# Mamba-2 scan and ELU feed-forward on one core: weight pieces spread over three steps, ELU first in each step, wide decays for two blocks, an earlier turn

## The chip, the cores and the metric

The kernel runs on one core of one Trainium2 chip. The metric is the device time of one execution in microseconds (us). Below, PE is the matrix engine (PEld its weight loads), DVE, ACT and POOL are the vector, scalar and GpSimd engines, and SP issues most DMAs.

## The reference

Two operations one after the other, in float32. The first is a chunked state-space scan over 4 batches, 8 heads, 768 tokens, head size 32 and state size 16; the second is a feed-forward layer with ELU over 3072 tokens (256 to 2048 to 256):

```python
cum = np.cumsum(la, axis=-1)                      # la = log(a) in one chunk
L = np.exp(cum[:, :, :, None] - cum[:, :, None, :]) * causal
M = np.einsum('bhin,bhjn->bhij', Cc, Bc) * L
y[:, :, sl] = einsum(M, xc) + einsum(Cc, state) * np.exp(cum)[..., None]
state = decay_full * state + sum over j of Bc_j xc_j * decay_from_j
...
x = y.transpose(0, 2, 1, 3).reshape(3072, 256)
h = x @ w_in
g = np.where(h > 0.0, h, np.exp(np.minimum(h, 0.0)) - 1.0)
out = g @ w_out
```

The two weights reach the kernel as 64-bit floats, and it makes 32-bit ones of them itself.

## The kernel before

**Blocks.** The 3072 tokens are 12 blocks of 256 (`n` = 0 to 11), each with all 8 heads of a batch. Inside a block the scan goes by chunks of 64 tokens. All four engines' orders are written out by hand: an instruction stands in its engine's queue where the Python text emits it, and nothing reorders it.

**The scan of a block** has these parts: `spread_cum` (a DMA puts the running sums of `log a` into the tile `L`, two buffers), `decay_of` (L516: per head two ACT exponentials of 128x64 with a bias from `ncum`, the negative running sum by token; after four heads two POOL selects cut the half above the diagonal away), `scaled` (POOL: B times its decay), `turn` (L421: four transposes on PE, one copy on ACT, then on DVE the masked C, `ctm`) and `turn_exp` (DVE), `scores` (PE, four PSUM tiles), `sums` (PE, two PSUM tiles), `weigh` (DVE: M = scores times `L`), `states` (DVE steps `S_new`, each followed by a POOL product `Sx`), `across` (PE, from `Sx`) and `inside` (PE, from M and x; then six copies into `yT`, the layer's input).

**The layer.** Blocks 0 to 3 go through `l1(n, i)` (L655): four passes that make two hidden tiles of 128 features times 256 tokens in one PSUM tile. `elu()` (L682) takes the oldest of these: `Relu` and `Exp` on ACT (L680, L687), then one DVE operation that writes `g` (L689). The PSUM tile is free when that has run. `l2(n, j)` (L817) multiplies `g` with `w_out`. From hidden tile 8 of blocks 2 and 3 on, pairs of blocks go through `l1_words(n, m)` (L778), in which inputs and weights are split in words (`words_of_y`, `both_of_y`, `words_of_w`, `low_of_w`): six passes into two PSUM tiles, `high` (from y1 and y0) and `both` (from `y_both`), and the second layer is done by `second`, a generator that `l2s(count)` advances.

**PSUM.** Seven of eight banks belong to one pool, whose tiles are handed out in the order of the text; which released tile a new one takes, and so what PE waits for, follows from that order.

**Weight pieces.** There are 16 (0 to 7 are `w_in`, 8 to 15 are `w_out`). Each goes through `w_abs` (ACT), `w_low` (ACT or DVE), `w_sign` (DVE), `w_high` (two DVE operations, L231 and L238) and `w_sum` (POOL, L248). `w_take` is the first three, `w_give` the last two.

**The two loops that the change rewrites.** The twelve-step loop (L1092 to L1134, `s` = 0 to 11) runs `l1(1, 0..7)` and `l1(0, 4..7)`, makes pieces 5 to 10 (each whole at one odd step, its `w_low` on DVE), exponentiates block 2's decays one head per step, turns block 2 at step 5, takes its scores and sums at step 7 and its `across` and `inside` at step 10, and calls `elu()` at the end of each step for the tile of the step before. The eight-step loop (L1173 to L1221, `j` = 0 to 7) runs `l2(0, j)` and `l1(2, 0..3)`, then `l1(3, 0..3)`, makes pieces 11 to 15 (one a step at j = 0, 2, 3, 4, 5: `w_take` before `l1`, `w_give` after it, then `elu()`), finishes block 3 (states at j = 2, `across` at j = 3) and begins blocks 4 and 5 (`scan_ahead`). It ends with `words_of_y(2)` at j = 4 and `both_of_y(2)` at j = 5. A loop of `l1_words(2, 8..15)` follows, and then one of 16 steps for each pair from block 4 on.

Of the kernel before, what the change touches and what calls it, by code (L numbers as in the profile page):

```python
# [17 lines left out]
P = 128  # L18
Q = 64
# [13 lines left out]
def kernel(  # L33
# [406 lines left out]
    def turn_exp(n, eng=nc.vector):  # L440

        s = st[n]
        s["cts"] = s["squares"][:, 1]
        eng.tensor_tensor(out=s["cts"], in0=s.pop("ct"), in1=s["ec"], op=ALU.mult)
# [68 lines left out]
    def decay(n, q):  # L513

        decay_of(n, 2 * q)
        decay_of(n, 2 * q + 1)  # L516

    def decay_of(n, h):
        L, row = st[n]["L"], rows_of(n).start + NG * h
        for u in range(2):  # L520
            nc.scalar.activation(  # L521
                L[:, h, u], L[:, h, u], ACT.Exp, bias=ncum[:, u, row:row + 1])
        if h % 4 == 3:
            for v in range(2):
                part = L[Q * v:Q * v + Q, h - 3:h + 1]
                nc.gpsimd.affine_select(  # L526
                    out=part, in_=part, pattern=[[0, 4], [0, 2], [1, Q]],
                    compare_op=ALU.is_ge, fill=0.0, base=0, channel_multiplier=-1)

# [218 lines left out]
    def words_of_y(n):  # L750

        y = yT[n // 2].rearrange("p k b u i -> p k (b u i)")
        y1 = conv.tile([P, KC, 2 * BLK], F32R, tag="y1", name="y1", bufs=1)
        y0 = conv.tile([P, KC, 2 * BLK], F32R, tag="y0", name="y0", bufs=1)
        nc.scalar.activation(y1[:, 1], y[:, 1], ACT.Copy, scale=NEAR / WORD)
        if n == 4:
            nc.scalar.activation(y1[:, 0], y[:, 0], ACT.Copy, scale=NEAR / WORD)
        else:
            nc.vector.tensor_scalar(
                out=y1[:, 0], in0=y[:, 0], scalar1=NEAR / WORD, scalar2=None, op0=ALU.mult)  # L760
        for k in range(KC):
            nc.vector.scalar_tensor_tensor(
                out=y0[:, k], in0=y1[:, k].bitcast(F32), scalar=WORD, in1=y[:, k],
                op0=ALU.mult, op1=ALU.subtract)
        y_words[n] = y1, y0
# [11 lines left out]
    def l1_words(n, m, between=None):  # L777

        cols = slice(m % 2 * P, (m % 2 + 1) * P)
        w, w0 = k_words[m // 2]  # L780
        w1, both_w, w0 = w[:, 0, :, cols], w[:, 1, :, cols], w0[:, :, cols]
        y1, y0, both_y = y_words[n]
        high, both = psum([P, 2 * BLK], "ps_h"), psum([P, 2 * BLK], "ps_w")
        passes = [(high, w1, y1), (high, w0, y0), (both, both_w, both_y)]
        for ps, lhs, rhs in passes if n > 2 and m == 0 else passes[2:] + passes[:2]:
            for k in range(KC):
                nc.tensor.matmul(  # L787
                    out=ps, lhsT=lhs[:, k], rhs=rhs[:, k], start=k == 0 and lhs is not w0,
                    stop=k == KC - 1 and lhs is not w1)
        if between:  # L790
            words_of_y(between)
        e = ffn.tile([P, 2 * BLK], F32, tag="e", name="e", bufs=2)
        nc.scalar.activation(e, both, ACT.Copy, scale=WORD)  # L793
        if late:
            end_words()
        nc.vector.scalar_tensor_tensor(  # L796
            out=high, in0=high, scalar=WORD - 1.0, in1=e, op0=ALU.mult, op1=ALU.add)
        late.append((n, m, high, e))
# [167 lines left out]
    def w_take(i, low):  # L966

        w_abs(i)
        w_low(i, low)
        w_sign(i)  # L970

    def w_give(i):

        w_high(i)
        w_sum(i)
# [112 lines left out]
    w_load(10)  # L1088
    write_flat(2)

    todo = 5
    for s, (n, i) in enumerate((  # L1092
            (1, 0), (1, 1), (1, 2), (0, 4), (1, 3), (0, 5), (1, 4), (0, 6), (1, 5), (0, 7),
            (1, 6), (1, 7))):
        l1(n, i, parts=2 if s < 2 else 1)
        if s < 8:
            decay_of(2, s)
        if s == 7:
            st[0] = kept
            scores(2)  # L1100
            sums(2, 0, pool=p_o, tag="o", parts=(None, last))
            weigh(2, 0)
            weigh(2, 1)
        if s % 2 == 1 and todo < 11:
            w_take(todo, nc.vector)
            w_give(todo)
            w_load(todo + 6)
            todo += 1
        if s in (1, 3):
            load_bc(3, us=(s // 2,))  # L1110
        if s == 9:
            write_flat(0)
        if s == 4:
            scaled(2, nc.gpsimd)
        if s == 5:
            turn(2)
            turn_exp(2)
        if s == 4:
            load_x(3)
            spread_exp(3)  # L1120
        if s == 8:
            weigh(2, 2)
            weigh(2, 3)
            states(0, last)
            st.pop(0)
            states(2)
        if s == 9:
            decay(3, 0)
            decay(3, 1)
        if s == 10:  # L1130
            spread_cum(4)
            inside(across(2), 2)
        if len(lag) > 1:
            elu()  # L1134


    def weigh_two(m, q):
# [35 lines left out]
    for j in range(2 * DIRECT):  # L1173
        n, i = 2 + j // DIRECT, j % DIRECT
        if j < 7:
            l2(0, j)
        piece = todo < len(pieces) and j != 1
        if j == 0:
            elu()
        if piece:  # L1180
            w_take(todo, nc.vector)
        l1(n, i)
        if j == 7:
            l2(0, j)
        if j == 0:
            scaled(3, nc.gpsimd)
            turn(3)
            elu()
            turn_exp(3)
        if piece:  # L1190
            w_give(todo)
            todo += 1
        while lag:
            elu()
        if j == 0:
            decay(3, 2)
            decay(3, 3)
        if j == 1:
            scores(3)
            sums(3)  # L1200
            for q in range(4):
                weigh(3, q)
        if j == 2:
            states(3)
        if j == 3:
            inside(across(3), 3)
        if j == 4:
            words_of_y(2)
        if j == 4:
            words_of_w(4)  # L1210
        if j == 5:
            low_of_w(4)
        if j == 5:
            both_of_y(2)
        scan_ahead(j)
        if j == 3:
            s_out[:] = weight_sums()
        if j == 6:
            differences(0, 4)
        if j == 7:  # L1220
            words_of_w(5)  # L1221
    for j in range(8, 16):
        i = j - 8
        l1_words(2, j)
        if i == 7:
            words_of_y(4)
        for p in ((), (6,), (), (7,), (0,), (1,), (2,), ())[i]:
            words_of_w(p)
        for p in ((5,), (), (6,), (7,), (0,), (), (), ())[i]:
            low_of_w(p)  # L1230
        if i == 7:
            l2(1, 6)
            l2(1, 7)
        begin_end()
        if i == 0:
            turn_part(5, 2)
            scaled(4, nc.gpsimd)
            scaled(5, nc.gpsimd)
        if i < 2:
            load_bc(i + 6)  # L1240
            l2(1, i)
        if i == 2:
            turn_part(4, 3)
            turn_part(5, 3)
            scores(4, 5)
            sums(4, 5)
            for q in range(4):
                weigh_two(4, q)
            l2(1, 2)
            states(4)  # L1250
            states(5)
            for to in (6, 7):
                load_b(to)
                spread_cum(to)
        if i == 3:
            l2(1, 3)
        if i == 4:
            y = across(4, 5)
            l2(1, 4, half=0)
            inside(y, 4, 5, ts=(0,))  # L1260
            l2(1, 4, half=1)
            inside(y, 4, 5, ts=(1,))
        if i == 5:
            l2(1, 5)
        if i in (0, 1, 3, 4):
            sum_t1(2, (0, 1, 3, 4).index(i), nc.vector)
        if i in (4, 6):
            turn_part(6, i // 2 - 2)
        if i in (2, 5):
            differences(4 if i == 2 else 6, 2)  # L1270
        if i < 6:
            sum_weights(nc.gpsimd, a_out, s_out, i)
# [30 lines left out]
    for n in range(4, NP, 2):  # L1303
# [3 lines left out]
        def l2s(count):  # L1307
            for _ in range(count):
                next(steps)

        for k in range(16):
# [13 lines left out]
            if not m:  # L1325
                l2s(4 if k % 2 else 3)
                continue
            l2s((3 + (n == 4), 3 - (n == 4), 3, 3, 3, 3, 3, 3, 4, 5, 2, 2, 3, 1, 2, 0)[k])
            if k == 9:
                scores(m, m + 1)  # L1330
                sums(m, m + 1)
# [5 lines left out]
                states(m + 1)  # L1337
            if k == 13:
                y = across(m, m + 1)
                l2s(1)  # L1340
                inside(y, m, m + 1, ts=(0,))
                l2s(2)
                inside(y, m, m + 1, ts=(1,))
        if m:
            l2s(4)
# [39 lines left out]
```

## Time and profile before

| what | us |
|---|---|
| median of 3 runs (349.99 to 350.6) | 350.07 |
| the profiled execution, its own time | 350.85 |
| its span | 349.1 |
| PE busy | 339.9 |
| DVE / ACT / POOL busy | 259.0 / 234.7 / 216.8 |
| twelve-step loop and the one product after it, 27.5 to 53.7: span, PE, ACT busy | 26.2, 26.19, 24.04 |
| from there to the end of step j = 7's `l1`, 53.7 to 81.5: span, PE, ACT busy | 27.8, 27.80, 23.87 |
| words of blocks 2 and 3, 81.5 to 117.7: span, PE, DVE busy | 36.2, 34.56, 32.35 |

Times in the profile count from the start of the span. A row of the timeline gives start and duration in us, then engine, line, operation, written tile <- read tiles, sizes and how many such instructions were merged; in square brackets, how long the engine sat idle before, and what ended that. Durations of neighbouring instructions of one engine overlap a little, so the distance from start to start (the pitch) is what one costs in a full queue.

### The profile page before, as it was taken

To read this page: it belongs to the slowest core of one execution; us is meant where nothing else is said; L and a number is where in the kernel's file an instruction comes from. 1 tells how busy PE (TensorE), PEld (TensorE's weight loads), DVE (VectorE), ACT (ScalarE), POOL (GpSimd) and SP (SyncE) were. 2 spreads that over 40 slices of the span, in tenths; PEclk is the share of its full clock that TensorE was granted. 3 is DMA by queue.
4 is the path that set the end of the run, shared out by engine and by line. 5 is a ranking of instruction groups with operands and counts; after the bars stand their busy time and mean duration, and the time that the engine had idled before them with its cause. 6 is when DMAs were issued, how large, how long until landed. Compare 5 with 4: busy or idle time off the path is not lost.

```text
span 349.1 us, 9873 instructions
## 1 busy us (share of the span) xinstructions
PE 339.9 (97%) x3878; PEld 297.5 (85%) x3878; DVE 259.0 (74%) x515; ACT 234.7 (67%) x537; POOL 216.8 (62%) x338
## 2 busy tenths in 40 slices
PE   7889999998999999999999999999999999999996
PEld 4669888887777889988999988989988999999996
DVE  4898988879997889875878775888675756665232
ACT  5689989597748889657699447699557466565000
POOL 5554554566999599984196764196854174455760
PEclk9999999999999999999999999999999999999999
DMA  8878988470261331070431070320000100001002
GB/s 145 220 220 180 303 175 252 95 132 31 66 126 23 91 62 32 8 151 15 106 62 32 8 160 4 99 40 2 2 0 5 62 0 3 0 0 56 9 0 62
DMA packets 72727, 26.49 MB, mean 76 GB/s; under 512 B 57768, under 2 KB 67560, under 8 KB 72680
## 3 DMA queue, kind: packets, MB, share of 16 engines
q1 hardware_dynamic: 70360, 25.60, 31.4%
q8 instruction: 30, 0.49, 0.6%
q10 hardware_dynamic: 2320, 0.26, 0.5%
q14 instruction: 17, 0.14, 0.1%
HBM read 22.51 MB, written 3.34 MB: 74 GB/s over the span
## 4 chain that ended last, share of the span: by engine, by line
PE 87%; DVE 3%; DMA 3%; SPq 3%; ACT 1%; issue 1%; POOL 1%; DVEq 0%; POOLq 0%; ACTq 0%
PE ps_o L904 36%; PE ps_h L787 18%; PE ps_h L667 11%; PE ps_w L787 9%; PE ps_o L829 6%; PE ps_y L634 3%; DMA w<-in_moe_w_in_dram 2%; PE ps_g L541 2%; PE ps_y L616 2%; PE ps_st L571 1%; DMA bc<-in_C_dram 1%; DVE y_both L772 1%; SPq L116 1%; SPq L178 1%; PE ps_o L890 1%
## 5 line engine op out<-in xcount | busy, mean ns | idle before, releaser
L904 PEld LDWEIGHTS ps_o<-w_out,g 128*128 128x128 f32 x640 | 78.5, 191 | 3.5
L904 PE MATMUL ps_o<-w_out,g 128*128 128x128 f32 x640 | 80.1, 275 | 0.0
L802 ACT ACTIVATE e<-ps_h 128x512 f32<-128x512 f32 x72 | 43.0, 598 | 50.5 <-DVE ps_h L796 50.5
L810 DVE SCALAR_TENSOR_TENSOR g<-e,ps_h 128x512 f32<-128x512 f32 x72 | 49.3, 685 | 31.1 <-ACT e L803 30.8
L845 POOL TENSOR_TENSOR g<-g 128x256 f32<-128x256 f32 x36 | 26.5, 737 | 57.3 <-DVE g L810 57.2
L796 DVE SCALAR_TENSOR_TENSOR ps_h<-ps_h,e 128x512 f32<-128x512 f32 x72 | 50.1, 695 | 13.1 <-ACT e L793 10.0
L793 ACT ACTIVATE e<-ps_w 128x512 f32<-128x512 f32 x72 | 42.3, 587 | 15.0 <-PE ps_w L787 14.9
L787 PE MATMUL ps_w<-y_both,w_words 128*128 128x512 f32 x144 | 51.5, 437 | 0.1
L667 PE MATMUL ps_h<-yT,w_in 128*128 128x256 f32 (+1 forms) x208 | 45.2, 368 | 2.5 <-POOL w_in L248 1.6
L803 ACT ACTIVATE e<-e 128x512 f32<-128x512 f32 x72 | 45.5, 632 | 2.3
L787 PE MATMUL ps_h<-y,w_words 128*128 128x512 f32 x144 | 45.6, 398 | 0.0
L787 PE MATMUL ps_h<-y,w 128*128 128x512 f32 x144 | 45.0, 392 | 0.2 <-POOL w L845 0.2
L667 PEld LDWEIGHTS ps_h<-yT,w_in 128*128 128x128 f32 x208 | 36.3, 190 | 8.4 <-POOL w_in L248 3.6
L521 ACT ACTIVATE L<-L,ncum 128x64 f32<-128x64 f32 x160 | 42.2, 336 | 0.2
L904 PE MATMUL ps_o<-w_sum,g 128*128 128x128 f32 x304 | 38.6, 276 | 0.0
L904 PEld LDWEIGHTS ps_o<-w_sum,g 128*128 128x128 f32 x304 | 37.0, 192 | 1.3
L526 POOL TENSOR_SCALAR_AFFINE_SELECT L<-L 64x512 f32<-64x512 f32 x40 | 29.2, 731 | 9.6 <-ACT L L521 7.5
L787 PEld LDWEIGHTS ps_h<-y,w 128*128 128x128 f32 x144 | 27.0, 188 | 7.1 <-POOL w L845 0.7
L787 PEld LDWEIGHTS ps_h<-y,w_words 128*128 128x128 f32 x144 | 26.7, 188 | 6.2 <-issue 0.5
L829 PE MATMUL ps_o<-w_out,g 128*128 128x256 f32 x128 | 30.9, 384 | 1.0 <-POOL w_out L248 1.0
L845 POOL TENSOR_TENSOR g<-t,g 128x256 f32<-128x256 f32 x40 | 28.1, 734 | 5.8 <-PE ps_o L904 5.7
L845 POOL TENSOR_TENSOR g<-g,t 128x256 f32<-128x256 f32 x40 | 28.7, 747 | 0.2
(133 smaller groups left out, 535.9 us busy)
## 6 DMA issues: line engine op xcount, KB each, us to landing
L<-flat SPq DMA_DIRECT2D x20, 256.0 KB
w<-in_moe_w_out_dram SPq DMA_DIRECT2D x8, 512.0 KB
w<-in_moe_w_in_dram SPq DMA_DIRECT2D x7, 512.0 KB
xr<-in_x_dram SPq DMA_DIRECT2D x24, 128.0 KB
out_dram<-c_sum SPq DMA_DIRECT2D x9, 256.0 KB
bc<-in_B_dram SPq DMA_DIRECT2D x24, 64.0 KB
bc<-in_C_dram SPq DMA_DIRECT2D x22, 64.0 KB
ec<-flat_exp SPq DMA_DIRECT2D x10, 128.0 KB
```

The source lines that it names most:

```text
L521: nc.scalar.activation(L[:, h, u], L[:, h, u], ACT.Exp, bias=ncum[:, u, row:row + 1])
L526: nc.gpsimd.affine_select(out=part, in_=part, pattern=[[0, 4], [0, 2], [1, Q]], compare_op=ALU.is_ge, fill=0.0, base=0, channel_multiplier=-1)
L667: nc.tensor.matmul(out=ps[:, j, toks], lhsT=w_in[i][:, k, j * P:(j + 1) * P], rhs=yT[n // 2][:, k, n % 2].rearrange("p u i -> p (u i)")[:, ...
L787: nc.tensor.matmul(out=ps, lhsT=lhs[:, k], rhs=rhs[:, k], start=k == 0 and lhs is not w0, stop=k == KC - 1 and lhs is not w1)
L793: nc.scalar.activation(e, both, ACT.Copy, scale=WORD)
L796: nc.vector.scalar_tensor_tensor(out=high, in0=high, scalar=WORD - 1.0, in1=e, op0=ALU.mult, op1=ALU.add)
L802: nc.scalar.activation(e, high, ACT.Relu, scale=-1.0)
L803: nc.scalar.activation(e, e, ACT.Exp, scale=-1.0)
L810: nc.vector.scalar_tensor_tensor(out=g_of[n, m].rearrange("p b i -> p (b i)"), in0=e, scalar=1.0, in1=h, op0=ALU.subtract, op1=ALU.max)
L829: nc.tensor.matmul(out=o_of[n][:, ts], lhsT=g_of[n, j][:, m % 2, ts * P:(ts + 1) * P], rhs=w_out[:, m], start=(m == 0 and ts == 0), stop=( ...
L845: nc.gpsimd.tensor_tensor(out=out, in0=in0, in1=in1, op=ALU.subtract)
L904: nc.tensor.matmul(out=ps[:, ts], lhsT=b[:, ts * P:(ts + 1) * P], rhs=a[:, i], start=(i == chunk[0] and ts == 0), stop=(i == chunk[-1]), s ...
```

## The change

It edits eight places:

- Pieces 5 to 10 are spread over three steps: `w_abs` and `w_sign` at an even step, `w_low` (on ACT instead of DVE) and `w_high` at the next, `w_sum` at the one after.
- In the twelve-step loop `elu()` comes right behind `l1`, ahead of everything else of the step.
- Blocks 2 and 3 get their decays in halves of four heads: a POOL addition of `ncum` over 128x512 (`from_token`), one ACT exponential of 128x512 (`wide_exp`), and the two POOL selects (`mask`), each a step apart. Block 2's run from before step 0 to step 3, block 3's from step 7 to 11.
- Block 2's `turn` and `turn_exp` move from step 5 to step 4, behind `scaled`.
- In the eight-step loop pieces 11 to 15 come whole behind `elu()`, with `w_low` on ACT; piece 15 moves from j = 5 to j = 4.
- `words_of_y` has both halves of y1 on ACT for n = 2 as well as n = 4.
- `l1_words` does `both` last at m = 15 and, for n = 2, at m = 8; `words_of_y(4)` moves into `l1_words(2, 15)`, ahead of its evacuation.
- Some `l2` and `l2s` calls around `inside` are regrouped; their number stays.

```diff
+    def from_token(n, half, eng=nc.gpsimd):
+        part = st[n]["L"][:, 4 * half:4 * half + 4]
+        first_row = rows_of(n).start + 4 * NG * half
+        eng.tensor_tensor(
+            out=part, in0=part,
+            in1=ncum[:, :, first_row:first_row + 4 * NG:NG].rearrange(
+                "p u h -> p h u").unsqueeze(3).to_broadcast([P, 4, 2, Q]), op=ALU.add)
+    def wide_exp(n, half):
+        part = st[n]["L"][:, 4 * half:4 * half + 4]
+        nc.scalar.activation(part, part, ACT.Exp)
...
-        nc.scalar.activation(y1[:, 1], y[:, 1], ACT.Copy, scale=NEAR / WORD)
-        if n == 4:
-            nc.scalar.activation(y1[:, 0], y[:, 0], ACT.Copy, scale=NEAR / WORD)
-        else:
+        for k in (0, 1) if n < 6 else (1,):
+            nc.scalar.activation(y1[:, k], y[:, k], ACT.Copy, scale=NEAR / WORD)
+        if n > 5:
...
-        for ps, lhs, rhs in passes if n > 2 and m == 0 else passes[2:] + passes[:2]:
+        for ps, lhs, rhs in passes if m == (8 if n == 2 else 0) or m == 15 else passes[2:] + passes[:2]:
...
+    def step(s):
+        for n, at in ((2, -1), (3, 7)):
+            for half in range(2):
+                if s == at + 2 * half + 2:
+                    mask(n, half)
+                if s == at + 2 * half:
+                    from_token(n, half)
+                if s == at + 2 * half + 1:
+                    wide_exp(n, half)
+    def convert(s):
+        p = 5 + s // 2
+        if s % 2 == 0 and s > 0:
+            w_sum(p - 1)
+        if s % 2 == 0 and p < 11:
+            w_abs(p)
+            w_sign(p)
+        if s % 2 == 1:
+            w_low(p, nc.scalar)
+            w_high(p)
+            w_load(p + 6)
+    step(-1)
...
         l1(n, i, parts=2 if s < 2 else 1)
-        if s < 8:
-            decay_of(2, s)
+        if len(lag) > 1:
+            elu()
+        step(s)
...
-        if s % 2 == 1 and todo < 11:
-            w_take(todo, nc.vector)
-            w_give(todo)
-            w_load(todo + 6)
-            todo += 1
+        if s == 4:
+            scaled(2, nc.gpsimd)
+            turn(2)
+            turn_exp(2)
+        convert(s)
...
-        if s == 9:
-            decay(3, 0)
-            decay(3, 1)
...
-        if len(lag) > 1:
-            elu()
...
         if j == 0:
+            w_sum(10)
             elu()
-        if piece:
-            w_take(todo, nc.vector)
         l1(n, i)
...
-        if piece:
-            w_give(todo)
-            todo += 1
         while lag:
             elu()
-        if j == 0:
-            decay(3, 2)
-            decay(3, 3)
+        for p in {0: (11,), 2: (12,), 3: (13,), 4: (14, 15)}.get(j, ()):
+            w_take(p, nc.scalar)
+            w_give(p)
...
-        l1_words(2, j)
-        if i == 7:
-            words_of_y(4)
+        l1_words(2, j, between=4 if i == 7 else None)
...
-            l2(1, 4, half=0)
             inside(y, 4, 5, ts=(0,))
-            l2(1, 4, half=1)
+            l2(1, 4)
...
-                l2s(1)
                 inside(y, m, m + 1, ts=(0,))
-                l2s(2)
+                l2s(4)
```

In the last loop the entry for k = 14 in the list of `l2s` counts goes from 2 to 1.

## The prediction

> **What bounds the kernel now.** I read the page first, then what PE waited for, then the timeline of each stretch that the change touches. The page gives PE 97% busy and 87% of the chain that ended last, and PEclk 9 in every slice. So the end moves only by what PE waits, and the wait list says how little that is.
>
> ```profile
> PE 87%; DVE 3%; DMA 3%; SPq 3%; ACT 1%; issue 1%; POOL 1%; DVEq 0%; POOLq 0%; ACTq 0%
> PE ps_h L667 <- POOL w_in L248: 1.6, 3, 0.8
> PE ps_o L829 <- POOL w_out L248: 1.0, 1, 1.0
> ```
>
> All three waits for `w_in` end by 23.3 us, ahead of the change. From 27.5 on the only long one is 1.0 us for piece 15 of `w_out`. The change can win that and a few tenths more; it loses whatever new wait it makes. So I put the new order of each queue against PE's pace: 1.73 us for an `l1` or an `l2` (53.72 to 55.45 in PE's timeline).
>
> The twelve-step loop, timeline of all engines (ACT's rows from 14 us for `w_low`):
>
> ```profile
> 16.13 0.74 ACT L205 ACTIVATE w_in<-w,two 128x512 f32<-128x512 uint32 x1
> 16.77 0.58 ACT L680 ACTIVATE e<-ps_h 128x512 f32<-128x512 f32 x1
> ...
> 28.10 0.63 ACT L687 ACTIVATE e<-e 128x512 f32<-128x512 f32 x1
> 28.72 1.27 POOL L248 TENSOR_TENSOR w_in<-mag,w_in 128x512 uint32<-128x512 uint32 x1 [2.82 <-DVE mag L238]
> 28.87 1.06 ACT L521 ACTIVATE L<-L,ncum 128x64 f32<-128x64 f32 x4
> ...
> 33.66 0.67 ACT L196 ACTIVATE mag<-w 128x512 f32<-128x512 f32 x1
> 34.23 0.58 ACT L680 ACTIVATE e<-ps_h 128x512 f32<-128x512 f32 x1
> 34.84 0.63 ACT L687 ACTIVATE e<-e 128x512 f32<-128x512 f32 x1
> 35.38 0.57 ACT L521 ACTIVATE L<-L,ncum 128x64 f32<-128x64 f32 x2
> 35.85 0.58 ACT L680 ACTIVATE e<-ps_h 128x512 f32<-128x512 f32 x1
> ...
> 43.53 5.05 PEld L667 LDWEIGHTS ps_h<-yT,w_in 128*128 128x128 f32 x24 [0.17 <-DVE M L550]
> ```
>
> ACT has no hole here: each row starts where the one before lets it. The pitches are `w_abs` 0.57 (33.66 to 34.23), `Relu` 0.62, `Exp` of 512 columns 0.54 (34.84 to 35.38), two narrow exponentials 0.48, `w_low` on ACT 0.64 (16.13 to 16.77). ACT runs some 2 us behind PE, and PE does not feel it yet.
>
> The eight-step loop around block 3's states, and around piece 14:
>
> ```profile
> 65.70 1.28 POOL L248 TENSOR_TENSOR w_out<-mag,w_out 128x512 uint32<-128x512 uint32 x1 [2.67 <-DVE mag L238]
> 66.93 1.41 POOL L593 TENSOR_TENSOR Sx<-S_new,hmask 128x64 f32<-128x64 f32 x4
> 67.62 0.66 PEld L616 LDWEIGHTS ps_y<-bct,Sx 32*64 32x64 f32 x32 [0.33 <-POOL Sx L593]
> ```
>
> ```profile
> 73.62 0.69 DVE L238 SCALAR_TENSOR_TENSOR mag<-mag,sgn 128x512 uint32<-128x512 uint32 x1
> 74.46 1.28 POOL L248 TENSOR_TENSOR w_out<-mag,w_out 128x512 uint32<-128x512 uint32 x1 [1.39 <-DVE mag L238]
> ...
> 81.59 2.58 DVE L772 SCALAR_TENSOR_TENSOR y_both<-y,yT 128x512 fp32r<-128x512 f32 x2
> 82.44 2.32 POOL L845 TENSOR_TENSOR w<-w_in,w_words 128x256 fp32r<-128x256 f32 x2
> 82.54 1.99 PE L829 MATMUL ps_o<-w_out,g 128*128 128x256 f32 x8 [1.02 <-POOL w_out L248]
> ```
>
> POOL's `Sx` come behind piece 12's sum and just in time; piece 14 is ready at 75.74 for an `l2(0, 6)` that starts at 76.17. Both margins are under half a us.
>
> **The twelve-step loop, part by part.** *from_token* has no row. Its bounds are twice the 128x256 product with a broadcast factor (L408, 0.63 to 0.83, so 1.26 to 1.66); I take 1.28, the two-input POOL operation of the same size (L248). The first cannot start before 29.99, behind piece 4's sum in POOL's queue (28.72 + 1.27), and ends at 31.27. Behind it on ACT stands `wide_exp`, and everything else of the loop behind that: ACT, free at 28.64 (28.10 + 0.54), idles 2.7 us, where before it went on at 28.87. *wide_exp* replaces eight narrow exponentials (1.95) by one of 0.54, the pitch of the same-sized `Exp`. *w_low* adds 0.64 to ACT per piece and frees 0.42 to 0.66 of DVE (L209), which isn't the limit. Over the stretch these cancel: block 2's 16 narrow ones and half of block 3's (24 x 0.24 = 5.8) go, four wide ones and six `w_low` (2.2 + 3.8 = 6.0) come. So ACT keeps its load, and the 2.7 us of late start stay as lag.
>
> With these pitches, from `wide_exp` at 31.33: `Relu` of (1,0) at 32.44 (before 30.41), of (1,2) at 36.52, of (0,5) at 42.14, of (1,4) at 43.87 (six `elu` at 1.16, two wide, four `w_abs`, three `w_low`, one copy of 0.27: 12.54 in all). `g` of (1,4) is then written at 43.87 + 0.62 + 0.63 + 0.7 = 45.8.
>
> Who waits for that has changed as well. Before, `l1(1, 5)` took the PSUM tile that `weigh` had freed (the 0.17 at 43.53). With `elu` ahead of `weigh` in the text, it takes the tile of (1,4), two steps old, and waits for its `g`; `sums(2)` waits for that of (0,5), 44.1. PE, which would be there at about 43.5, goes on at 45.9. The smaller waits before it (piece 6's sum ends at 40.84 for a step that starts at 40.5) are inside this one. After it PE runs at its pace: three `l1`, block 2's `across` and `inside` (1.3), `l1(1, 7)` and `l2(0, 0)` put `l1(2, 0)` at 45.9 + 5.2 + 1.3 + 3.5 = 55.9 against 53.72. **+2.2 us.** Turning block 2 a step sooner costs nothing: its B and C have landed by 31.6 and it needs them at 36.3. DVE's added queue is hidden behind ACT, whose `Exp` comes later each time.
>
> **The eight-step loop.** Piece 12 now stands whole behind `elu` at j = 2, and `states(3)` behind it. Count from T, the end of `l1(2, 2)` (64.07 before): `Relu` T+0.2, `Exp` +0.82, `w_abs` +1.36 to +2.03, DVE's `g` to +2.1, then sign, limits and L238 to +3.6, POOL's sum +3.65 to +4.9, and only then the four `Sx` at 0.35 each. `across(3)` needs the second at +5.65; before it started at +3.55 (67.62). **+2.1 us.** What waits behind: `inside(3)`, `l2(0, 4)` and all of PE.
>
> Piece 14 is alike, with T' the end of `l1(3, 0)` (72.72 before): its `w_abs`, before at 72.48 and ahead of that `elu`, now follows it; the sum ends at T'+4.92, and `l2(0, 6)` comes at T'+3.46, two products later. **+1.45 us.** Pieces 10, 11, 13 and 15 have 1 us or more left by the same count. ACT is free in time: its eight narrow exponentials before (70.55 to 72.48) hang on `inside(3)`, as does T'.
>
> **What it wins.** Piece 15 starts a step sooner, so the 1.02 at 82.54 goes. `y_both`, done at 84.17 just when it was wanted, gets 0.93 us more by the new order of passes at m = 8 and a DVE without the first half of y1 (1.12) and two `w_low`: no new wait. **-1.0 us.** With m = 15's order, words and evacuation only change places on DVE; the 0.30 and 0.42 that PE waits for `y_both` near 117 may go or stay: I take 0, bounds -0.5 and +0.3. The regrouped `l2s` have 1.3 us or more of products on either side: 0, bounds 0.3 either way over four pairs.
>
> DVE's pair for `y_both` takes 2.58 at 81.59, beside POOL's L248 and L845, and 1.28 at 168.19, alone. The Trainium skill (page "SBUF — State Buffer", section "Who interferes with whom") says that a DVE instruction with two SBUF inputs and a POOL one that reads SBUF share a port, and the second blocks until the first is done. These rows agree. By it each `from_token` may hold such an instruction for its whole length; it is the rival of contention below.
>
> **The sum.** 2.2 + 2.1 + 1.45 - 1.0 = +4.7 us; the profiled span of 349.1 would be 353.8. The profiled execution took 350.85 in all, 0.8 above the median, so I set the difference on the median: 350.07 + 4.7 = **354.8 us**.
>
> **Rivals.**
> *Only the twelve-step loss is real* (the queues of j = 2 and 4 slip past by some cover that I don't see). For it: both margins there are short counts of rows; against: POOL and DVE take their queues in order. 350.07 + 2.2 - 1.0 = 351.3.
> *Faster: ELU first keeps PSUM ahead of PE.* Place: the tiles that PE reuses in the twelve steps. If `g` of (1,4) is written by 43.5 and the second `Sx` by T+3.5, no wait is added, and the waits at 43.53 (0.17), 48.9 (0.33), 82.54 (1.02) and near 117 (0.7) go: 350.07 - 2.2 = 347.9. It needs ACT 2.3 us earlier than my count, so a `from_token` of no length or a hole in ACT's queue, and the rows show neither.
> *Cancelled*: the loop loses about 1 us (PE less bound to `g` than the order of PSUM tiles says) and 82.54 gives it back: 350.1.
> *Contention*: `from_token` at 1.66, and one DVE instruction of the late chains held for a POOL operation's 1.3, as at 81.59: 354.8 + 0.4 + 1.3 = 356.5.
>
> **Chances.** The forecast (within 1 us or so) 0.58; only the twelve-step loss 0.16; contention 0.11; faster 0.09; cancelled 0.06. Two tenths of a per cent, 0.7 us, is about what a measurement of this kernel can tell from no change; so faster 0.09, same 0.06, slower 0.85. The range leaves out faster and cancelled and goes to the contention case: 351.0 to 356.6.
>
> **What would show it.** In the changed profile: ACT idle about 2.5 us before the first `wide_exp`, released by POOL; PE waiting near 44 to 46 for DVE's `g`; PE's `across(3)` waiting about 2 us for POOL's `Sx`, behind a sum of `w_out`; PE waiting 1 to 1.5 us for POOL's `w_out` at `l2(0, 6)` and not at `l2(0, 7)`; from `l1_words(2, 8)` on the same distances as before. I am wrong if PE goes through the twelve steps without idle time, or if the two waits of the eight-step loop are missing.

## The result, and the profile after

The changed kernel takes 355.86 us (median of 5 runs, 355.51 to 357.46) where the kernel before, run beside it, takes 350.15 (349.99 to 350.71): a ratio of 1.0167, with a 95% interval from 1.0147 to 1.0186. It is slower by 5.7 us; the forecast was 354.8. The profiled execution took 355.51 us, with a span of 353.4.

First the chain that ended last, from the page of the changed kernel, in shares of the span:

```profile
PE 74%; POOL 6%; DVE 6%; ACT 5%; SPq 3%; DMA 3%; issue 2%; POOLq 0%; DVEq 0%; ACTq 0%
```

PE held 87% of it before. POOL, ACT and DVE have entered it, so some of PE's steps now begin when one of those is done. The list of PE's waits names them (what PE needed, who ended the wait; us in total, how often, the longest):

```profile
PE ps_h L683 <- POOL w_in L248: 2.5, 4, 0.9
PE ps_y L632 <- POOL Sx L609: 1.9, 1, 1.9
PE ps_o L844 <- POOL w_out L248: 1.5, 1, 1.5
...
PE ps_h L683 <- DVE g L705: 1.0, 1, 1.0
```

The twelve-step loop, timeline of the changed kernel (start, duration, engine, line, instruction, number; idle time before in brackets; rows of other work in between are left out here and below). L683 is now `l1`, L696 and L703 `Relu` and `Exp`, L705 `g`, L223 the sign, L522 `from_token`, L529 `wide_exp`, L632 `across`, L667 the copies to `yT`:

```profile
27.04 9.20 PE L683 MATMUL ps_h<-yT,w_in 128*128 128x128 f32 x56
...
29.48 1.25 POOL L522 TENSOR_TENSOR L<-L,ncum 128x512 f32<-128x512 f32 x1
30.76 0.63 ACT L529 ACTIVATE L<-L 128x512 f32<-128x512 f32 x1 [2.49 <-POOL L L522]
...
40.78 1.99 PE L683 MATMUL ps_h<-yT,w_in 128*128 128x256 f32 x8 [0.56 <-POOL w_in L248]
...
43.28 0.58 ACT L696 ACTIVATE e<-ps_h 128x512 f32<-128x512 f32 x1
43.50 1.05 DVE L223 TENSOR_SCALAR sgn<-w 128x512 uint32<-128x512 uint32 x1
43.90 0.63 ACT L703 ACTIVATE e<-e 128x512 f32<-128x512 f32 x1
44.56 0.69 DVE L705 SCALAR_TENSOR_TENSOR g<-e,ps_h 128x512 f32<-128x512 f32 x1
45.30 5.45 PE L683 MATMUL ps_h<-yT,w_in 128*128 128x256 f32 x24 [1.01 <-DVE g L705]
...
50.68 0.81 PE L632 MATMUL ps_y<-bct,Sx 32*64 32x64 f32 x32
...
52.70 1.37 POOL L522 TENSOR_TENSOR L<-L,ncum 128x512 f32<-128x512 f32 x1
54.10 0.63 ACT L529 ACTIVATE L<-L 128x512 f32<-128x512 f32 x1 [3.70 <-POOL L L522]
55.20 1.63 ACT L667 COPY yT<-ps_y 128x128 f32<-128x128 f32 x6
56.05 2.40 PE L683 MATMUL ps_h<-yT,w_in 128*128 128x256 f32 x8
56.88 1.16 PEld L683 LDWEIGHTS ps_h<-yT,w_in 128*128 128x128 f32 x6 [0.54 <-ACT yT L667]
```

ACT idles 2.49 us before the first wide exponential, and `l1(1, 5)` at 45.30 waits for the `g` that ends just before it: both as forecast. The last five rows were not forecast. Block 3's second `from_token` comes late, ACT waits 3.70 us for it, the copies to `yT` stand behind that exponential, and `l1(2, 0)` takes 2.40 us instead of 1.89. It reads what these copies write: its first two weight loads go at 56.05, half-way through the copies, and the rest at 56.88, as the last copy ends (55.20 + 1.63 = 56.83).

The eight-step loop, same timeline:

```profile
70.63 1.27 POOL L248 TENSOR_TENSOR w_out<-mag,w_out 128x512 uint32<-128x512 uint32 x1 [5.34 <-ACT L L541]
71.85 1.23 POOL L609 TENSOR_TENSOR Sx<-S_new,hmask 128x64 f32<-128x64 f32 x4
72.45 0.71 PE L632 MATMUL ps_y<-bct,Sx 32*64 32x64 f32 x32 [1.93 <-POOL Sx L609]
...
81.22 1.29 POOL L248 TENSOR_TENSOR w_out<-mag,w_out 128x512 uint32<-128x512 uint32 x1 [3.40 <-DVE mag L238]
82.57 1.99 PE L844 MATMUL ps_o<-w_out,g 128*128 128x256 f32 x8 [1.48 <-POOL w_out L248]
```

Piece 12's sum, then the `Sx`, then `across(3)`, 1.93 us late; piece 14's sum, then `l2(0, 6)`, 1.48 us late.

From here on, the measure is stretches from start to start on PE. The changed kernel's rows at 27.04 and 56.05 are shown above; the other ends are these, first of the kernel before, then of the changed one:

```profile
27.50 10.93 PE L667 MATMUL ps_h<-yT,w_in 128*128 128x128 f32 x64
53.72 1.89 PE L667 MATMUL ps_h<-yT,w_in 128*128 128x256 f32 x8
84.18 0.82 PE L787 MATMUL ps_w<-y_both,w_words 128*128 128x512 f32 x2
```

```profile
89.39 0.81 PE L802 MATMUL ps_h<-y,w_words 128*128 128x512 f32 x2
```

| stretch | before | after | difference |
|---|---|---|---|
| `l1(1, 0)` to `l1(2, 0)`, the twelve steps | 26.22 | 29.01 | +2.79 |
| `l1(2, 0)` to the first pass of `l1_words(2, 8)`, the eight steps | 30.46 | 33.34 | +2.88 |
| from there to the end of the span | 264.92 | 264.01 | -0.91 |

The loss, 5.67 us, lies in the first two. The last stretch is between 263.8 and 265.4 in all 14 profiled executions of this study, with the late edits and without; its -0.91 is inside that scatter. So is the start of `l1(1, 0)`, 0.46 us sooner in the changed kernel and between 26.49 and 27.72 in the 14. Because of these two, the profiled spans differ by only 4.3 us, and that 5.67 comes so near to the medians' 5.7 is in part chance.

One thing more is needed to read the times. Two of the changed kernel's five runs (357.21 and 357.46) had a mean granted clock of 0.995, the other three (355.51 to 355.86) one of 1.0. Of the 56 runs of the kernel before beside the experiments, one had 0.995 or less. The next section shows what it is.

### The profile page after: what moved, and what is told of

Same layout as the page of the kernel before. It is cut to its first block, busy times and chain, and to the rows that moved or that the text cites. A ratio compares the mean times of both kernels' runs of the same rounds, so it can differ in the third digit from the quotient of the medians.

```text
span 353.4 us, 9854 instructions
## 1 busy us (share of the span) xinstructions
PE 340.5 (96%) x3878; PEld 297.1 (84%) x3878; DVE 256.6 (73%) x503; ACT 237.0 (67%) x521; POOL 223.4 (63%) x342
## 4 chain that ended last, share of the span: by engine, by line
PE 74%; POOL 6%; DVE 6%; ACT 5%; SPq 3%; DMA 3%; issue 2%; POOLq 0%; DVEq 0%; ACTq 0%
PE ps_o L919 35%; PE ps_h L802 18%; PE ps_w L802 9%; PE ps_o L844 4%; DMA w<-in_moe_w_in_dram 3%; PE ps_h L683 2%; POOL L L534 2%; PE ps_y L650 2%; SPq L132 2%; PE ps_g L557 1%; PE ps_y L632 1%; PE ps_st L587 1%; DVE sgn L223 1%; ACT e L696 1%; DVE mag L238 1%
## 5 line engine op out<-in xcount | busy, mean ns | idle before, releaser
L683 PE MATMUL ps_h<-yT,w_in 128*128 128x256 f32 (+1 forms) x208 | 45.9, 369 | 3.9 <-POOL w_in L248 2.5
L683 PEld LDWEIGHTS ps_h<-yT,w_in 128*128 128x128 f32 x208 | 36.0, 190 | 10.9 <-POOL w_in L248 4.1
L534 POOL TENSOR_SCALAR_AFFINE_SELECT L<-L 64x512 f32<-64x512 f32 x40 | 30.7, 767 | 8.1 <-ACT L L541 6.0
L541 ACT ACTIVATE L<-L,ncum 128x64 f32<-128x64 f32 x128 | 33.8, 338 | 0.0
```

What stands on the lines that cost most here:

```text
L534: nc.gpsimd.affine_select(out=part, in_=part, pattern=[[0, 4], [0, 2], [1, Q]], compare_op=ALU.is_ge, fill=0.0, base=0, channel_multiplier=-1)
L541: nc.scalar.activation(L[:, h, u], L[:, h, u], ACT.Exp, bias=ncum[:, u, row:row + 1])
L683: nc.tensor.matmul(out=ps[:, j, toks], lhsT=w_in[i][:, k, j * P:(j + 1) * P], rhs=yT[n // 2][:, k, n % 2].rearrange("p u i -> p (u i)")[:, ...
```

## The experiments

Each kernel was timed in 5 rounds against the kernel before. "Low clock" counts the runs with a mean granted clock of 0.995 or less. The stretches are those of the table above, from the profiled execution; * marks one with such a low clock inside it. A run's time holds 1.7 to 3.7 us outside the profiled span, and runs of one kernel at a clock of 1.0 differ by up to 2.8 us. The stretches are free of the first.

| kernel | median us | ratio to before, 95% interval | low clock | twelve steps | eight steps |
|---|---|---|---|---|---|
| changed | 355.86 | 1.0167 (1.0147 to 1.0186) | 2 of 5 | 29.01 | 33.34 |
| e1_states_first | 355.45 | 1.0137 (1.0111 to 1.0163) | 0 of 6 | 28.97 | 32.64 |
| e2_piece14_early | 355.57 | 1.0138 (1.0114 to 1.0162) | 5 of 5 | 29.00 | 33.27* |
| e3_both | 354.0 | 1.0093 (1.0071 to 1.0115) | 0 of 6 | 28.96 | 30.88 |
| e4_late_only | 350.1 | 0.9977 (0.9961 to 0.9993) | 0 of 12 | 26.23 | 29.58 |
| f1_low_on_dve | 357.12 | 1.0192 (1.0173 to 1.0211) | 0 of 4 | 29.64 | 33.34 |
| f2_narrow | 356.99 | 1.0183 (1.0163 to 1.0203) | 1 of 4 | 29.18 | 33.13 |
| f3_elu_first | 351.2 | 1.0017 (1.0004 to 1.0031) | 0 of 12 | 26.71 | 30.95 |
| f4_wide_only | 354.42 | 1.0111 (1.0092 to 1.0129) | 1 of 5 | 30.15 | 30.45 |
| g1_block3_sooner | 357.34 | 1.0179 (1.0145 to 1.0212) | 3 of 6 | 28.52 | 32.83 |
| g2_weigh_first | 355.81 | 1.0148 (1.0120 to 1.0175) | 6 of 6 | 27.31 | 34.91* |
| g3_first_on_dve | 356.39 | 1.0143 (1.0108 to 1.0178) | 4 of 6 | 28.31 | 34.78* |
| g4_all | 355.24 | 1.0130 (1.0088 to 1.0172) | 2 of 6 | 31.13* | 30.14 |

### The two waits of the eight steps

e1 puts block 3's states ahead of piece 12; e2 takes piece 14 ahead of `l1(3, 0)` and gives it ahead of `elu`; e3 does both.

```diff
+        if j == 2:
+            states(3)
         for p in {0: (11,), 2: (12,), 3: (13,), 4: (14, 15)}.get(j, ()):
...
-        if j == 2:
-            states(3)
```

```diff
+        if j == 4:
+            w_take(14, nc.scalar)
         l1(n, i)
+        if j == 4:
+            w_give(14)
...
-        for p in {0: (11,), 2: (12,), 3: (13,), 4: (14, 15)}.get(j, ()):
+        for p in {0: (11,), 2: (12,), 3: (13,), 4: (15,)}.get(j, ()):
```

> The changed kernel with states(3) ahead of piece 12 at j = 2; nothing else differs. Theory (queues): DVE and POOL take their queues in order, so the wait of across(3) for Sx (1.93 us of PE idle, 2.3 of PEld) falls to 0.4 or less, and the time is 1.6 to 2.1 us under the changed kernel's 355.9, near 354.0. l2(0, 4) then comes 2 us sooner and may wait for piece 12 up to 0.5 us. Rival (lateness only): PE arrives late from the twelve steps whatever happens here and the wait moves on to piece 12 or 14; time within 0.5 us of 355.9.

> The changed kernel with piece 14 taken before l1(3, 0) and given ahead of elu, as in the kernel before; piece 15 stays behind elu at j = 4. Theory (queues): the 1.48 us that PE waits for w_out at l2(0, 6) goes, piece 15 is ready by l2(0, 7), and the time is 1.3 to 1.6 us under 355.9, near 354.4. Rival (DVE is full here: its instructions beside POOL took 1.5 and 2.4 us at 81 to 86): the wait moves to l2(0, 7) or to y_both, and less than 0.6 us is won.

> Both of the moves above in the changed kernel. Theory: they add up, 3.0 to 3.6 us under 355.9, near 352.6; PE then waits for nothing between 58 us and the first words of blocks 2 and 3, and what is left of the loss, some 2.8 us against 1.0 won for piece 15, is the twelve-step loop's. Rival: one wait hides the other, and the sum is under 2.2 us.

PE's waits for pieces of `w_out` and for `Sx` in e1 (first fence) and in e3 (second):

```profile
PE ps_o L844 <- POOL w_out L248: 2.9, 2, 1.5
```

```profile
PE ps_o L844 <- POOL w_out L248: 1.4, 1, 1.4
```

In both, the wait for `Sx` is gone from the list. Yet e1 won only 0.70 us in the eight steps, against a theory of 1.6 to 2.1: piece 12's sum, now behind the states, is late for `l2(0, 4)`, so most of the 1.93 came back as a second wait for `w_out`, as the rival said. In e3 piece 14's wait is gone as well and only piece 12's is left (1.4). The eight steps are 2.46 us shorter, and the median is 1.7 below the changed kernel's three runs at a clock of 1.0: more than in e1 or e2, less than the 3.0 to 3.6 of its theory.

e2 removes the 1.48 and shows no gain where 1.3 to 1.6 was forecast. Its rival, a wait that moves on, is not in its list; here the clock comes in. Busy time by engine in windows of 2 us; the third field from the right is the granted clock. First e2, then the changed kernel:

```profile
72.00:74.00 2.00, 1.23 (x91) 1.12 (x94) 1.80 (x4) 1.42 (x4) 1.40 (x5) 1.00 1.12 213
74.00:76.00 2.00, 2.00 (x33) 1.63 (x18) 2.00 (x3) 1.90 (x8) 1.27 (x1) 0.68 0.75 124
76.00:78.00 2.00, 2.00 (x6) 1.56 (x5) 0.11 (x1) 2.00 (x8) 1.20 (x2) 0.50 0.61 95
78.00:80.00 2.00, 2.00 (x10) 1.74 (x10) 1.12 (x2) 1.18 (x3) 0.59 (x2) 0.97 0.34 53
```

```profile
74.00:76.00 2.00, 2.00 (x10) 1.77 (x11) 0.65 (x2) 1.91 (x8) 1.27 (x1) 1.00 0.76 123
76.00:78.00 2.00, 2.00 (x11) 1.77 (x10) 0.00 (x0) 1.65 (x7) 1.33 (x2) 1.00 0.19 27
```

Some 2 us behind the wait for `Sx`, which ends at 72.77, e2's PE goes to half its clock for some 3.4 us (1.28 + 2.0 + 0.12, each window's missing share over the half) and loses 1.7 us: about as much as piece 14 was worth. In the profiled execution of the changed kernel the clock stays at 1.0; its two runs at 0.995 are 1.4 to 2.0 us longer than the other three, about the same size, but no trace of them shows where their clock fell.

### The late edits alone

e4 is the kernel before with the edits from `words_of_y` on: the orders of passes at m = 8 and 15, y1 on ACT for n = 2, `words_of_y(4)` inside `l1_words(2, 15)`, the regrouped `l2` and `l2s`.

```diff
-        for ps, lhs, rhs in passes if n > 2 and m == 0 else passes[2:] + passes[:2]:
+        for ps, lhs, rhs in passes if m == (8 if n == 2 else 0) or m == 15 else passes[2:] + passes[:2]:
...
-        l1_words(2, j)
-        if i == 7:
-            words_of_y(4)
+        l1_words(2, j, between=4 if i == 7 else None)
```

> The kernel before with only the late edits: the order of passes at m = 8 and 15, words_of_y on ACT for n = 2 and inside l1_words for n = 4, and the regrouped l2 and l2s. Theory from the two traces (from the first product of second to the end 231.4 us before, 230.3 after): each pair's gap around inside shrinks by 0.2 to 0.5 us, 0.5 to 1.1 us in all, so 349.0 to 349.6; the wait of 1.02 for piece 15 stays. Rival: the two executions differ by chance there, and the time is within 0.3 us of the kernel before.

It is the only version faster than both kernels: 350.1 against 350.63 beside it, by the ratio some 0.8 us (0.2 to 1.4). The place of the gain is not the one that was forecast: the theory kept the 1.0 us wait at `l2(0, 7)`, and it is no longer on e4's list, while the eight steps are 0.88 shorter. Piece 15 stands where it stood, but its sum comes 0.9 us sooner, as the words of y were taken off DVE (the piece's first DVE operation starts at 77.40 instead of 79.29). It ends at 81.11, for an `l2(0, 7)` that starts at 81.16, 0.1 us behind the product before it. e4's row, which the kernel before has at 81.22 with `l1(1, 0)` half a us later:

```profile
79.83 1.28 POOL L248 TENSOR_TENSOR w_out<-mag,w_out 128x512 uint32<-128x512 uint32 x1 [1.49 <-DVE mag L238]
```

So that wait was not only a matter of the step at which piece 15 was begun.

### What makes the twelve steps longer

f1 and f2 undo one part of the change each (`w_low` of pieces 5 to 10 back on DVE; narrow decays). f3 and f4 do one part alone on the kernel before (`elu` right behind `l1`; wide decays).

```diff
-            w_low(p, nc.scalar)
+            w_low(p, nc.vector)
```

```diff
-    step(-1)
...
-        step(s)
+        if s < 8:
+            decay_of(2, s)
+        if s == 9:
+            decay(3, 0)
+            decay(3, 1)
...
+        if j == 0:
+            decay(3, 2)
+            decay(3, 3)
```

```diff
         l1(n, i, parts=2 if s < 2 else 1)
+        if len(lag) > 1:
+            elu()
...
-        if len(lag) > 1:
-            elu()
```

```diff
+    step(-1)
...
-        if s < 8:
-            decay_of(2, s)
+        step(s)
...
-        if s == 9:
-            decay(3, 0)
-            decay(3, 1)
...
-        if j == 0:
-            decay(3, 2)
-            decay(3, 3)
```

> The changed kernel with w_low of pieces 5 to 10 back on DVE; rest as changed. Theory (ACT is full and its lag is what PE meets): by the Relu of (1,4) three w_low of 0.7 are gone from ACT's queue, its g is written 2 us sooner, at about 43.2, and PE no longer waits 1.01 us for it at l1(1, 5) nor 0.56 for piece 6; what stays is the late wide_exp of block 3 ahead of the copies into yT. Time 1.4 to 2.0 us under 355.9. Rival (DVE and POOL block each other: sign took 1.05 to 1.21 beside from_token, 0.42 alone): DVE gets 0.4 to 0.9 more per piece and the time falls by less than 0.6 us or rises.

> The changed kernel with the narrow decays of the kernel before for blocks 2 and 3 (one head a step behind elu; block 3's at s = 9 and j = 0); rest as changed. Theory: no from_token, so ACT does not idle 2.5 us at 28.2 nor 3.7 us before block 3's second wide_exp, but it has 8 x 0.48 us more to do by step 8; the Relu of (1,4) comes at 43.0 against 43.28, PE still waits for its g, and of the loss in the twelve steps only the 0.6 us at l1(2, 0) goes and 0.3 at l1(1, 5): 0.5 to 1.2 us under 355.9. Rival (the late start alone is the loss): 2.2 us or more under 355.9.

> The kernel before with only elu moved right behind l1 in the twelve steps. Theory (order of PSUM tiles): l1(1, 5) and sums(2) now take tiles that elu frees two steps earlier in the text instead of those that weigh frees; ACT, full as before, writes g of (1,4) at about 44.0 against the 43.5 at which PE wants the tile: PE waits 0.3 to 0.8 us there, and the time is 0.2 to 0.8 us over 350.15. Rival (ELU first lets PE run ahead): 0.2 us or more under 350.15.

> The kernel before with only the wide decays (from_token, wide_exp, mask, at the steps of the change) for blocks 2 and 3. Theory: ACT idles 2.5 us before the first wide_exp but has 5.8 - 2.2 = 3.6 us less to do and no w_low, so it has caught up by step 7; elu still last, PSUM tiles as before. PE loses at most 0.6 us, from block 3's second half on POOL behind Sx; from_token also stands ahead of the pieces' sums on POOL, 1.25 us each, with margins of 1 us or more. Time 350.1 to 350.9. Rival (from_token is the cost): 1.5 us or more over 350.15.

From `l1(1, 0)` to `l1(1, 5)` PE takes 16.04 us before, 18.26 changed, 18.89 in f1, 18.19 in f2, 16.55 in f3 and 18.03 in f4. ELU first alone costs half a us, as much as its theory said but not where: f3's PE waits at `scores(2)`, for the masked C that DVE writes (`ctm`), and not at `l1(1, 5)` for a `g`. Wide decays alone cost 2.0 up to there, against a theory of 0.6 at most for the whole stretch, and most of it arises at `scores(2)` too, which starts 1.2 us later than before and takes 1.51 us. The rows of `scores(2)`, in f3 and then in f4 (0.69 us and no wait in the kernel before):

```profile
41.70 1.00 PE L541 MATMUL ps_g<-ctm,bct 32*64 32x128 f32 x32 [0.19 <-DVE ctm L436]
```

```profile
42.44 1.51 PE L561 MATMUL ps_g<-ctm,bct 32*64 32x128 f32 x32 [0.84 <-DVE ctm L436]
```

Undoing the wide decays in the changed kernel gives 0.1 back: f2's ACT has no idle time, but carries the narrow exponentials and six `w_low`. Its median, 356.99, lies above the changed kernel's although its two stretches together do not (62.31 against 62.35); no trace shows why, and the gain of 0.5 to 1.2 that was forecast is not there. So the parts do not add up: PE meets its wait at another product in f3 and f4 than in the changed kernel. In f1, where ACT has the least to do, it is DVE's queue that is late, as these rows of f1's timeline show:

```profile
43.84 1.28 POOL L248 TENSOR_TENSOR w_in<-mag,w_in 128x512 uint32<-128x512 uint32 x1 [2.59 <-DVE mag L238]
44.28 1.12 DVE L223 TENSOR_SCALAR sgn<-w 128x512 uint32<-128x512 uint32 x1
44.45 0.60 ACT L696 ACTIVATE e<-ps_h 128x512 f32<-128x512 f32 x1 [0.73 <-DVE g L705]
...
45.32 0.67 DVE L705 SCALAR_TENSOR_TENSOR g<-e,ps_h 128x512 f32<-128x512 f32 x1
```

The sign takes 1.12 us instead of 0.41, ending 0.28 behind POOL's sum. The `g` behind it is that of (1, 4), whose `Exp` was done at 43.73: it waits for DVE alone, and `l1(1, 5)` for it. ACT, too, waits for DVE. f1's rival, DVE beside POOL, held, though what the signs stand beside is the sum and not `from_token`; its theory fell.

f4 lost a further 1.9 us late in the loop, so its rival (1.5 us or more) held. Its timeline:

```profile
49.56 1.46 POOL L534 TENSOR_SCALAR_AFFINE_SELECT L<-L 64x512 f32<-64x512 f32 x2
51.11 1.10 POOL L522 TENSOR_TENSOR L<-L,ncum 128x512 f32<-128x512 f32 x1
52.25 0.63 ACT L529 ACTIVATE L<-L 128x512 f32<-128x512 f32 x1 [3.77 <-POOL L L522]
52.78 1.64 ACT L671 COPY yT<-ps_y 128x128 f32<-128x128 f32 x6
53.08 1.99 PE L687 MATMUL ps_h<-yT,w_in 128*128 128x256 f32 x8 [1.89 <-ACT yT L671]
```

This is the row that the changed kernel shows at 54.10, here at a higher price: mask and `from_token` late on POOL, the exponential behind them on ACT, the `yT` copies behind that, and PE waiting. Here it is `l1(1, 7)` that waits, for the PSUM tile that the first copy releases; in the changed kernel it is `l1(2, 0)`, for its input.

### Mending the twelve steps

Three single repairs of the changed kernel, and then all together with pieces 12 and 14.

```diff
-        for n, at in ((2, -1), (3, 7)):
+        for n, at in ((2, -1), (3, 6)):
```

```diff
-            w_sign(p)
+            if s < 6:
+                w_sign(p)
...
             w_low(p, nc.scalar)
+            if s > 6:
+                w_sign(p)
...
-        if len(lag) > 1:
+        if len(lag) > 1 and s != 7:
             elu()
...
             weigh(2, 1)
+            elu()
```

```diff
-                    from_token(n, half)
+                    from_token(n, half, nc.vector if s < 0 else nc.gpsimd)
```

> The changed kernel with block 3's wide decays one step sooner in the twelve steps (from_token at s = 6 and 8, the exponential at 7 and 9, the mask at 8 and 10). Theory: l1(2, 0) pays 0.6 us since its PSUM bank is freed by copies of yT that stand on ACT behind a wide exponential, which waits 3.70 us for a from_token that stands on POOL behind five Sx and a mask. With from_token ahead of the Sx that wait of ACT is gone, and the stretch from l1(1, 0) to l1(2, 0), 29.0 us, is 0.5 to 0.8 us shorter: 355.1 to 355.4 where the kernel before gives 350.15. Rival: the shared work of DVE and POOL decides, and from_token only meets other DVE instructions: no change within 0.3 us, or slower.

> The changed kernel with elu behind weigh at s = 7 alone, and the signs of pieces eight to ten on DVE in the odd steps, so that the sign (1.05 us at 43.50) is not ahead of M. Theory: l1(1, 5) waits till 45.30 for the tile of (1, 4) only because elu stands ahead of weigh; it takes weigh's tile now, free at about 44.1, and the 1.0 us goes: the changed kernel less 0.8 to 1.2 us, 354.7 to 355.1 where the kernel before gives 350.15. Rival: ACT's lag is what counts, and the next l1 waits for its g in place of this one, or across(2) for its Sx: less than 0.3 us is won.

> The changed kernel with the first from_token on DVE instead of POOL, behind g at about 29.15 and no longer behind piece 4's sum. Theory, as the prediction has it: the late start of ACT (2.5 us idle before the first wide exponential) stays as lag and shows at l1(1, 5) and before it. ACT starts 0.4 to 0.9 us sooner, the waits at 40.78 (0.56) and 45.30 (1.01) shrink by as much: the changed kernel less 0.4 to 0.9 us, 355.0 to 355.5 where the kernel before gives 350.15. Rival: the lag is not carried from there, since ACT with narrow decays and no idle time was no sooner at 43.7; then nothing changes, within 0.2 us.

In the twelve steps each won about what its theory said, or more: g1 -0.49 (ACT's 3.70 before the second exponential is gone and `l1(2, 0)` is back at 1.89), g2 -1.70, g3 -0.70 (ACT's first idle time is 0.65 shorter, and `l1(1, 5)` comes 0.68 sooner). In the medians none of it shows, and all three forecasts of the time were missed: 3, 6 and 4 of their 6 runs have the low clock, which the profiled executions of g2 and g3 show in the eight steps. g2's timeline, where `M` now runs ahead of `g`:

```profile
44.08 0.76 DVE L566 TENSOR_TENSOR M<-ps_g,L 128x256 f32<-128x256 f32 x2
44.79 5.45 PE L683 MATMUL ps_h<-yT,w_in 128*128 128x256 f32 x24
45.12 0.69 DVE L705 SCALAR_TENSOR_TENSOR g<-e,ps_h 128x512 f32<-128x512 f32 x1 [0.28 <-ACT e L703]
```

`l1(1, 5)` starts ahead of that `g`, with no wait: it was the order of the text, through the PSUM tile, that had tied it to (1, 4). In that stretch the theory holds, by the times it can't be told.

> The changed kernel with its five late places mended together and everything else of the change kept (elu first, pieces over three steps, wide decays): pieces 12 and 14 taken ahead of l1 and given behind it (w_low stays on ACT), elu behind weigh at s = 7 and the signs of pieces eight to ten in odd steps, block 3's wide decays a step sooner, the first from_token on DVE. Theory: the whole loss sits in waits that PE makes at these places. From the changed kernel's undisturbed executions, 355.5 to 355.9, go the wait for Sx (1.93), that for piece 14 (1.48), that for g of (1, 4) (1.01), that for piece 6's sum (0.56) and the one behind the late yT copies (0.5 to 0.8): 349.8 to 350.8 where the kernel before gives 350.1 to 350.6, and the granted clock stays at 1.0, since PE has no break of 3.4 us between full products near 72 us. Rival: the elements of the change that are kept (w_low on ACT, from_token on POOL beside DVE) cost time of their own, and another step waits in place of these: 351.5 or more.

The theory fell: 355.24 us, and 353.4 to 354.3 in the three runs whose clock was 1.0. Of the rival, the time and the other step that waits came true; the cause that it named, `w_low` on ACT and `from_token` beside DVE, is not what the rows show. `l1(1, 5)` comes 16.54 us behind `l1(1, 0)`, nearly as before, and the eight steps take 30.14; but a new wait stands between. g4's timeline:

```profile
43.79 1.06 POOL L522 TENSOR_TENSOR L<-L,ncum 128x512 f32<-128x512 f32 x1 [3.05 <-DMA L<-flat]
44.88 0.63 ACT L529 ACTIVATE L<-L 128x512 f32<-128x512 f32 x1 [1.46 <-POOL L L522]
...
46.69 0.69 DVE L705 SCALAR_TENSOR_TENSOR g<-e,ps_h 128x512 f32<-128x512 f32 x1 [2.40 <-ACT e L703]
...
51.19 1.56 POOL L609 TENSOR_TENSOR Sx<-S_new,hmask 128x64 f32<-128x64 f32 x5
52.17 0.88 PE L632 MATMUL ps_y<-bct,Sx 32*64 32x64 f32 x32 [2.32 <-POOL Sx L609]
...
53.97 3.32 PE L683 MATMUL ps_h<-yT,w_in 128*128 128x256 f32 x8
```

Block 3's `L` lands only at 43.8. `from_token`, a step sooner, waits for it at the head of POOL's queue, with ACT's exponential, `g`, and at last block 2's `Sx` behind it: 2.32 us. The next `l1` runs at half clock (3.32 us instead of 1.89). What was late is g1's edit, and not a part of the change that was kept. In g1 the same wait for the DMA was 1.83, and no wait of PE came of it, since PE was later there. Whether the mended steps without g1's edit would reach the kernel before was not tried.

## Why the prediction was right

*What bounds the kernel.* Right: PE's waits. The first two stretches, which hold them, give +5.67 us; the rest is scatter, and the medians' +5.7 agrees with it better than such scatter allows one to expect.

*Twelve steps, +2.2.* Measured +2.79. The chain forecast from `from_token` over ACT to `g` of (1, 4) held within 0.15 us: it put `l1(1, 5)` 18.4 us behind `l1(1, 0)`, and it came at 18.26. Its inner times held as well: counted from `l1(1, 0)`, the `Relu` of (1, 2), (0, 5) and (1, 4) came within 0.15 us of the forecast. g3 shows that the late start is carried forward (0.65 less idle, 0.68 sooner), g2 that the order of the text ties PE to that `g`. What was missed is the term behind `l1(1, 5)`: the working let PE run "at its pace" to `l1(2, 0)`, and did not ask what a second late `from_token` does to the copies of `yT` queued behind its exponential on ACT. That cost 0.26 ahead of `l1(2, 0)`, within the twelve steps, and 0.5 in it, within the eight. Block 2's `across`, at 0.81 us instead of 0.49 (48.91 before), is most of the rest; why it is slower no run shows.

*ACT's load cancels.* In keeping with the runs: f2, with narrow exponentials and `w_low` on ACT, reaches `l1(1, 5)` within 0.07 us of the changed kernel, so up to there the narrow ones cost ACT as much as the wide ones and the late start together. Of DVE the prediction said that its added queue is hidden behind ACT. That holds in the changed kernel, but not in f1, so the move of `w_low` to ACT was worth something.

*Piece 12 ahead of the states, +2.1.* `across(3)` came 5.54 us behind T, forecast 5.65; PE waited 1.93.

*Piece 14, +1.45.* PE waited 1.48.

*The win, -1.0.* The size is right and the reason not shown: all but 0.1 of the wait at `l2(0, 7)` is gone in e4 too, where piece 15 was not moved. So the earlier step may have been needed for that 0.1 or not at all, and that the sum has the right size here is in part luck.

*Regrouped `l2s` and m = 15, 0.* No run shows more: the last stretch differs by no more than the scatter, and a wait of 0.3 for `y_both` stays in e4 and in the changed kernel.

*The rivals.* "Only the twelve-step loss" is ruled out by the two waits and by e3. "Faster" and "cancelled" had ELU first keep PSUM ahead of PE; f3 shows that alone it costs 0.6 us (0.1 to 1.1 by its interval). "Contention" priced a DVE instruction held for a POOL operation: signs of 1.05 to 1.21 us are there (0.42 alone), beside the pieces' sums. Ahead of the `g` of (1, 4), which PE waits for, the sign ends at 44.55 and ACT's `Exp` at 44.53, so without the hold this `g` would have come no sooner than `Exp` let it. In f1 the hold does cost time. The forecast's missing us is mostly the late `yT` and the slower `across`. The half clock, which no rival had, has the size of what the two runs at 357 lost; that it caused them is not shown.

## What to carry to other kernels

When an instruction is moved, follow each queue past the first thing that waits: here the same `from_token` was late twice, and what stood behind its second exponential was the input of one of PE's products. Take a kernel's waits one at a time by undoing single edits, but read the gain in stretches from start to start, since a removed wait may return one product later (e1), or be hidden in the total time by a clock drop (e2, g2). A repair that moves work earlier has its bound in the transfer that feeds it: look up when the data land first (g4).

## What the runs showed of the hardware

**A wait of 2 us on PE can cost 3.6.** Behind the wait for `Sx` the clock goes to 0.50 for some 3.4 us in the traces of e2, g2 and g3, and behind another wait, of 2.32 us, in g4's. Spread over a span of 353 us such a drop makes a mean clock of 0.995. By that mean, 21 of the 36 runs of kernels with the 1.93 us wait for `Sx` had one or more, among them every run of e2 and g2 and two of five of the changed kernel, and none of the 12 of e1 and e3, where that wait is gone. The mean alone does not say where it fell or what it cost: f4's only run at 0.995 is its fastest. PE's empty time was only 1.93 us; but until the next full product came 1.45 us of 32- and 64-row products for `across` and `inside`, so the break between full products was 3.4 us (70.52 to 73.91 in the changed kernel). The Trainium skill (page "TensorE: Matmul & The Clock Gate", section "What's actually happening") gives a free-running window of 3.4 us and a clock that is either full or half, half after an idle window. The two levels and the length agree. A free-running window would also explain why a break of this length is caught in some runs and not in others, f1 among them (0 of 4 with the same 1.9 us wait); this was not tested. That small products count as little activity is inferred, and was not tested by itself.

**A sign beside a sum.** DVE's one-input 128x512 operation on `w` takes 0.42 us alone, and 1.21 in the changed kernel at 47.48, where it ends 0.3 us behind the sum that POOL began at 47.12 and ended at 48.39. The Trainium skill (page "SBUF — State Buffer", section "Who interferes with whom") says that such operations, too, can take the port pair shared with POOL, and that the second to come blocks until the first is done; these rows agree. The changed kernel's signs at 35.57 and 43.50 also end 0.3 us behind a sum. g2 moved the signs together with `elu`, so what the signs alone cost there is not shown.
